# Attention scores and weighted sums as 64-by-64 products on TensorE, and half of q transposed by products with the identity

## The chip, the cores and the metric

The kernel runs on one core of a Trainium2 chip. The metric is device time in microseconds (us), the median of several runs. The core's engines are named as in the profile: PE (TensorE, matrix products into PSUM), PEld (its weight loads, which overlap PE), DVE (VectorE), ACT (ScalarE), POOL (GpSimd), and SP, whose queue issues most DMAs.

## The reference

Everything is float32. Attention runs inside chunks of 64 tokens; its output feeds a layer with one of eight experts per token, and that feeds a last dense layer.

```python
def _attn_ref(q, k, v):                       # (8, 8, 576, 64) each
    q_c = q.reshape(B, H, nc, chunk, D)       # chunk = 64, nc = 9; k_c, v_c alike
    scores = scale * np.matmul(q_c, k_c.transpose(0, 1, 2, 4, 3))
    scores = scores - np.max(scores, axis=-1, keepdims=True)
    attn = np.exp(scores)
    attn = attn / (np.sum(attn, axis=-1, keepdims=True) + 1e-09)
    out = np.matmul(attn, v_c)

def reference(**kwargs):
    attn_out = _attn_ref(q, k, v)             # -> x: 4608 tokens of 512
    x = _moe_ref(x, w_gate, w1, w2)           # argmax of x @ w_gate picks 1 of 8 experts
    return _moe2_ref(x, w_in, w_out)          # (relu(x @ w_in) ** 2) @ w_out
```

## The kernel before

Three functions run in turn: `attention()` (to about 205 us of the profiled span), `experts()` (to about 685 us) and `second()`. The change touches the first alone. Its work is cut into 36 tiles of 128 tokens (two chunks), and into 18 units of two tiles, for which q and k are loaded together. A loop `for it in range(-4, NTILE + 1)` issues one tile's steps per turn, each for another tile: `scores(it + 1)`, the first half of the transposes of q or k (`trans(..., 0)`; q in even turns, k in odd ones), `x_t` (the transpose of a finished tile), `expo(it + 1)`, the second half (`trans(..., 1)`), `pv(it - 1)` (the weighted sum), `attn_t(it)`, and in some turns `late_steps`. Every engine takes its instructions in the order in which they are written, so this loop is the order of the work; semaphores hold an engine where its input is not there.

The steps, with the names of their tiles in the profile:

- `trans`: four 128x128 transposes on PE into a PSUM tile `tq`, one for each head; line 279 then copies `tq` to SBUF with four ACT copies of 64 partitions by 256 elements. q goes to `qT`, with two heads of a pair on the two halves of the partitions. k goes to `kb`, where every pair of heads is a block matrix with zeros in the two off-diagonal blocks; these are written once by `fill_k`.
- `scores`: eight products, 128 rows by 64 columns of weights from `qT`, 128 moving columns from `kb`, into `sc` (one PSUM bank; the pool `ps_s` holds two such tiles). The zeros keep the two heads of a pair apart. DVE then takes the maximum (`mx`, line 296) and subtracts it (`at`, line 298).
- `expo` and `attn_t`: ACT takes the exponential in place (line 303), PE transposes four times into `ta`, ACT copies to `aT` (line 311).
- `pv`: eight products of 128 rows, 64 columns and 130 moving columns, `aT` against `vb`, which again holds zeros (`fill_v`) and a column of ones for the sum, into `pv`. DVE adds 1e-9, takes the reciprocal and multiplies (lines 330 to 333); SP stores the tile to DRAM.
- `x_t`: four transposes into `tx`, a DVE copy to `xT` (line 349).
- `late_steps`: for every group of four tiles, in four turns, `gate` (PE products `gl`, ACT copy `gs`), `gate_t` and `route` (eight short DVE instructions), `place` (short PE products, DVE), and `scatter` (four indirect DMAs that POOL issues, line 510).

PSUM has eight banks: four tiles of `ps_t` (for `tq`, `tx`, `ta`, `gl` and others), two of `ps_s`, two for `pv`. SBUF is handed out by tags with a fixed number of buffers; the eight `vb` tiles take six of tag `h` and one each of `b` and `a`, so three of the four `a` buffers are left for loads of q and k.

## Time and profile before

| | us |
|---|---|
| median of 3 runs (lowest, highest) | 1479.04 (1475.89, 1479.36) |
| the profiled execution | 1477.98 |
| its span, first to last instruction | 1476.2 |
| attention: from 0 to the last transposes of its tiles | about 205 |

The span leaves 1.8 us of the profiled execution outside. The granted clock of TensorE has a mean of 0.995 of full speed. Over the whole span PE is busy 97%, DVE 51%, ACT 41%, POOL 32%; these shares are means over three stages with different limits, and attention has to be read for itself.

### The profile page before, as it was taken

How to read it: one execution, taken by the hardware profiler on the slowest of the kernel's cores; microseconds unless marked ns; L12 is line 12 of the kernel's file. 1: busy time of each engine (PE TensorE's matmuls, PEld its weight loads, DVE VectorE, ACT ScalarE, POOL GpSimd, SP SyncE). 2: the span in 40 equal slices, each digit the busy share in tenths (PEclk: the TensorE clock that was granted, in tenths of full speed). 3: DMA queues.
4: the chain of work that ended last, by engine and by line, in shares of the span. 5: the costliest groups of instructions: out<-in, count | busy, mean ns of one | idle time of the engine just before them, and what ended most of it. 6: DMA issues, size and time to landing. Idle time of an engine off the chain costs nothing.

```text
span 1476.2 us, 21686 instructions
## 1 busy us (share of the span) xinstructions
PE 1429.1 (97%) x8186; PEld 1219.6 (83%) x8186; DVE 757.4 (51%) x1374; ACT 601.0 (41%) x1111; POOL 468.7 (32%) x566
## 2 busy tenths in 40 slices
PE   6999978999999999999999999999999999999998
PEld 5777758888889999998888888888888888888886
DVE  4766767768887878885532232322233232322322
ACT  7988833443444445554432222222222222222222
POOL 5335455435545545653003040120403003040201
PEclk9999999999999999999999999999999999999999
DMA  9998645757767777885301010010101001010000
GB/s 202 262 216 208 171 130 183 217 171 228 235 210 232 238 229 256 260 269 179 107 1 59 0 60 0 24 36 0 59 0 52 8 8 52 1 59 1 30 2 29
DMA packets 144370, 172.91 MB, mean 117 GB/s; under 512 B 18160, under 2 KB 103872, under 8 KB 144256
## 3 DMA queue, kind: packets, MB, share of 16 engines
q1 hardware_dynamic: 110032, 112.58, 27.0%
q0 software_dynamic: 17920, 40.51, 9.8%
q10 hardware_dynamic: 16304, 18.36, 3.8%
q8 instruction: 66, 1.08, 0.3%
q14 instruction: 48, 0.39, 0.1%
HBM read 133.05 MB, written 38.34 MB: 116 GB/s over the span
## 4 chain that ended last, share of the span: by engine, by line
PE 53%; POOL 0%; POOLq 0%; issue 0%; DVE 0%
PE hp L993 27%; PE py L1014 26%; POOL out_dram L974 0%; POOLq L1079 0%; DVE o L1022 0%; POOL between L973 0%
## 5 line engine op out<-in xcount | busy, mean ns | idle before, releaser
L993 PE MATMUL hp<-xm,w_None 128*128 128x512 f32 x1728 | 416.5, 390 | 3.1 <-DVEq L937 3.1
L993 PEld LDWEIGHTS hp<-xm,w_None 128*128 128x128 f32 x1728 | 325.4, 188 | 71.0 <-ACTq L937 3.3
L1014 PE MATMUL py<-w_None,h 128*128 128x512 f32 x1512 | 363.2, 389 | 0.0
L1014 PEld LDWEIGHTS py<-w_None,h 128*128 128x128 f32 x1512 | 283.9, 188 | 58.8
L998 DVE SCALAR_TENSOR_TENSOR rs<-hp,rs 128x512 f32<-128x512 f32 x144 | 99.6, 691 | 435.0 <-ACT rs L997 431.6
L997 ACT ACTIVATE rs<-hp 128x512 f32<-128x512 f32 x144 | 85.9, 597 | 456.6 <-PE hp L993 446.0
L755 PE MATMUL pa<-xs,w 128*128 128x256 f32 (+2 forms) x1344 | 242.5, 329 | 6.9 <-DVE h L759 2.9
L767 PE MATMUL pb<-h,w 128*128 128x256 f32 (+2 forms) x1344 | 243.9, 331 | 0.0
L974 POOL DMA_INDIRECT out_dram<-o,tp x36 | 35.1, 974 | 628.6 <-ACT o L1020 622.6
L755 PEld LDWEIGHTS pa<-xs,w 128*128 128x128 f32 x1344 | 211.4, 189 | 24.7 <-DVE h L759 4.1
L767 PEld LDWEIGHTS pb<-h,w 128*128 128x128 f32 x1344 | 209.9, 190 | 14.5
L1000 DVE TENSOR_TENSOR h<-rs,h 128x512 fp32r<-128x512 f32 x144 | 99.7, 693 | 99.0 <-ACT h L999 95.5
L758 ACT ACTIVATE h<-pa 128x256 fp32r<-128x256 f32 (+2 forms) x112 | 53.2, 475 | 217.6 <-PE pa L755 169.9
L190 DVE TENSOR_TENSOR w<-raw,w 128x1024 fp32r<-128x1024 f32 x100 | 132.7, 1328 | 17.2 <-ACT w L189 12.4
L999 ACT CAST h<-rs 128x512 fp32r<-128x512 f32 x144 | 89.4, 621 | 111.2 <-DVE rs L998 100.2
L189 ACT CAST w<-raw 128x1024 fp32r<-128x1024 f32 x113 | 118.2, 1047 | 0.0
L759 DVE SCALAR_TENSOR_TENSOR h<-pa,h 128x256 fp32r<-128x256 f32 (+2 forms) x112 | 59.6, 535 | 61.5 <-ACT h L758 49.9
L803 POOL TENSOR_TENSOR cr<-cr 128x256 f32<-128x256 f32 x64 | 50.2, 784 | 124.5 <-ACT h L758 43.3
L804 POOL TENSOR_TENSOR cr<-cr 128x256 f32<-128x256 f32 x64 | 71.5, 1117 | 5.0
L258 POOL DMA_DIRECT2D vb<-in_v_dram x64 | 46.4, 747 | 67.4 <-PE pv L321 67.3
L270 PE MATMUL tq<-ident,qk 128*128 128x128 f32 x288 | 47.7, 296 | 14.1 <-DMA qk<-in_q_dram 9.9
L279 ACT COPY qT<-tq 64x256 f32<-64x256 f32 x144 | 56.0, 389 | 10.8 <-PE tq L270 9.1
(197 smaller groups left out, 1316.0 us busy)
## 6 DMA issues: line engine op xcount, KB each, us to landing
raw<-in_moe_w_dram SPq DMA_DIRECT2D x112, 512.0 KB
x_d<-x SPq DMA_DIRECT2D x36, 256.0 KB
x<-y_d POOLq DMA_DIRECT2D x36, 256.0 KB
cr<-in_moe_w_in_dram SPq DMA_DIRECT2D x32, 256.0 KB
cr<-in_moe_w_out_dram SPq DMA_DIRECT2D x32, 256.0 KB
vb<-in_v_dram POOLq DMA_DIRECT2D x56, 144.0 KB
qk<-in_q_dram SPq DMA_DIRECT2D x12, 512.0 KB
qk<-in_k_dram SPq DMA_DIRECT2D x12, 512.0 KB
```

What stands on the lines that cost most here:

```text
L189: nc.scalar.copy(w[0], raw)
L190: eng.tensor_tensor(out=w[1], in0=raw, in1=w[0], op=ALU.subtract)
L755: nc.tensor.matmul(ps[:, 0:N], lhsT=w[wl][:, kk, o:o + 128], rhs=xT[:, xl, kk, 0:N], start=(kk == 0 and wl + xl == 0), stop=(kk == KD - 1 ...
L759: nc.vector.scalar_tensor_tensor(out=h[:, 1, 0:N], in0=ps[:, 0:N], scalar=0.0, in1=h[:, 0, 0:N], op0=ALU.max, op1=ALU.subtract)
L767: nc.tensor.matmul(pb[d][:, 0:N], lhsT=w[wl][:, f % 2, 128 * d:128 * d + 128], rhs=h[:, hl, 0:N], start=(f + hl + wl == 0), stop=(f == NF ...
L804: nc.gpsimd.tensor_tensor(out=af, in0=af, in1=ef, op=ALU.add)
L993: nc.tensor.matmul(ps, lhsT=w[wl][:, kk, o:o + 128], rhs=xT[:, xl, kk, :], start=(kk == 0 and wl + xl == 0), stop=(kk == KD - 1 and wl == 1))
L997: nc.scalar.activation(out=rs[:, 0], in_=ps, func=AF.Relu)
L998: nc.vector.scalar_tensor_tensor(out=rs[:, 1], in0=ps, scalar=0.0, in1=rs[:, 0], op0=ALU.max, op1=ALU.mult)
L999: nc.scalar.copy(h[:, 0], rs[:, 1])
L1000: nc.vector.tensor_tensor(out=h[:, 1], in0=rs[:, 1], in1=h[:, 0], op=ALU.subtract)
L1014: nc.tensor.matmul(ys[t], lhsT=h[:, hl, 128 * t:128 * t + 128], rhs=w[wl][:, g % 2, :], start=(g == 0 and hl + wl == 0), stop=(g == NF2 - ...
```

## The change

The zeros go. `kb` keeps k transposed in the same layout as `qT`: two heads of a pair on the two halves of the partitions. `scores` then makes sixteen products instead of eight, each of 64 rows (one head), 64 columns and 64 moving columns; the two heads of a pair go to two PSUM banks, and `sc` becomes two banks large, with one buffer in place of two. `pv` makes sixteen products of 64 rows, 64 columns and 65 moving columns instead of eight with 130, the heads of a pair again in two banks. `vb` has four tiles, all of tag `h`, without the zero blocks.

For the first half of q (`one = nm == "q" and hh == 0`) the four transposes are replaced by eight products with the identity, each with 64 columns of weights; each lands on the half of the partitions on which its head belongs, so that one ACT copy of 128 partitions by 512 elements replaces the four. The other half of q, and k, are transposed and copied as before.

At the start, `fill_k` and `fill_v` (36 memsets of blocks of `kb` and `vb` on DVE and POOL) go; four POOL memsets of the columns of ones remain. v of the first batch is loaded in two parts of 2 and 7 chunks instead of 6 and 3, and the first part goes ahead of the second load of q and k. The load of v's second batch is written later (at `it == 0`), but on POOL's queue it still stands right behind that of the first.

```diff
-            ps_s = actx.enter_context(tc.tile_pool(name="ps_s", bufs=2, space=PSUM))
+            ps_s = actx.enter_context(tc.tile_pool(name="ps_s", bufs=1, space=PSUM))
...
-            vb = [[tl("hhhhhhba"[4 * s + p], [128, NCB, 2, D + 1], F32, f"vb{s}{p}") for p in range(NPAIR)] for s in range(2)]
-            kb = [tl("b", [128, NPAIR, 4, 2, CH], F32, f"kb{s}") for s in range(2)]
+            vb = [[tl("h", [128, 2, NCB, D + 1], F32, f"vb{s}{z}") for z in range(NPAIR // 2)] for s in range(2)]
+            kb = [tl("b", [128, NPAIR, 128, 2], F32, f"kb{s}") for s in range(2)]
...
+                one = nm == "q" and hh == 0
                 for h in range(4):
-                    nc.tensor.transpose(ps[:, h // 2, h % 2, :], src[:, 4 * hh + h, :], ident)
+                    if one:
+                        r, p = divmod(h, 2)
+                        for j in range(2):
+                            nc.tensor.matmul(ps[64 * j:64 * j + 64, p, r, :], lhsT=src[:, 2 * p + j, 64 * r:64 * r + 64], rhs=ident, start=True, stop=True)
+                    else:
+                        nc.tensor.transpose(ps[:, h // 2, h % 2, :], src[:, 4 * hh + h, :], ident)
+                to = st["qT", u] if nm == "q" else kb[u % 2]
+                if one:
+                    nc.scalar.copy(to[:, 2 * hh:2 * hh + 2].rearrange("q p n r -> q p r n"), ps)
+                    return
...
-                ps = ps_s.tile([128, H, CH], F32, tag="s", name="sc")
+                ps = ps_s.tile([128, 2, 512], F32, tag="s", name="sc")
                 for p in range(NPAIR):
                     for c2 in range(2):
...
+                        for j in range(2):
+                            c = slice(64 * h2 + 32 * c2, 64 * h2 + 32 * c2 + 32)
+                            nc.tensor.matmul(
+                                ps[64 * c2:64 * c2 + 64, j, CH * p:CH * p + CH],
+                                lhsT=qt[64 * j:64 * j + 64, p, c].rearrange("q i r -> q (i r)"),
+                                rhs=kt[64 * j:64 * j + 64, p, c].rearrange("q i r -> q (i r)"),
...
-                            ps[64 * c2:64 * c2 + 64, p // 2, o:o + 2 * (D + 1)],
-                            lhsT=aT[:, p, 64 * c2:64 * c2 + 64],
-                            rhs=vb[b % 2][p][:, c].rearrange("p j d -> p (j d)"),
...
+                        for j in range(2):
+                            nc.tensor.matmul(
+                                ps[64 * c2:64 * c2 + 64, j, (D + 1) * p:(D + 1) * (p + 1)],
+                                lhsT=aT[64 * j:64 * j + 64, p, 64 * c2:64 * c2 + 64],
+                                rhs=vb[b % 2][p // 2][64 * j:64 * j + 64, p % 2, c],
...
-            fill_k(0)
+            for s_ in range(2):
+                for t in vb[s_]:
+                    nc.gpsimd.memset(t[:, :, :, D:D + 1], 1.0)
+            load_v(0, (nc.gpsimd, nc.sync), 0, 2)
             load_qk(1)
...
-            fill_v(1, nc.gpsimd)
-            load_v(1)
...
+                if it == 0:
+                    load_v(1)
...
```

On PE, a turn of the loop in which q is transposed reads as follows before (`qk_286` is the loaded unit, `vb_106` to `vb_109` the four pairs of heads; a shape is weight columns by moving columns):

```order
L288 MATMUL sc<-kb_114,qT_312 64x128 x8
L270 MATMUL tq<-ident,qk_286 128x128 x4
L348 MATMUL tx<-ident,x 128x128 x4
L270 MATMUL tq<-ident,qk_286 128x128 x4
L321 MATMUL pv<-vb_106,aT 64x130 x2
L321 MATMUL pv<-vb_107,aT 64x130 x2
L321 MATMUL pv<-vb_108,aT 64x130 x2
L321 MATMUL pv<-vb_109,aT 64x130 x2
L309 MATMUL ta<-ident,at 128x128 x4
```

The same turn on PE now:

```order
L296 MATMUL sc<-kb_110,qT_286 64x64 x16
L276 MATMUL tq<-ident,qk_252 64x128 x8
L358 MATMUL tx<-ident,x 128x128 x4
L278 MATMUL tq<-ident,qk_252 128x128 x4
L331 MATMUL pv<-vb_106,aT 64x65 x8
L331 MATMUL pv<-vb_107,aT 64x65 x8
L319 MATMUL ta<-ident,at 128x128 x4
```

The order of the steps stays; the first `tq` series now has the 64-column shape and stands between two series of other shapes.

On ACT, two turns (q, then k) before:

```order
L279 COPY qT_530<-tq 64x256 x4
L303 ACTIVATE at<-at 128x512
L279 COPY qT_530<-tq 64x256 x4
L311 COPY aT<-ta 128x512
L279 COPY kb_114<-tq 64x8x32 x4
L303 ACTIVATE at<-at 128x512
L279 COPY kb_114<-tq 64x8x32 x4
L311 COPY aT<-ta 128x512
```

And now:

```order
L281 COPY qT_570<-tq 128x2x2x128
L313 ACTIVATE at<-at 128x512
L285 COPY qT_570<-tq 64x256 x4
L321 COPY aT<-ta 128x512
L285 COPY kb_110<-tq 64x256 x4
L313 ACTIVATE at<-at 128x512
L285 COPY kb_110<-tq 64x256 x4
L321 COPY aT<-ta 128x512
```

One copy stands where four stood, once in two turns; nothing else moves.

On SP's queue, at the start of the program, before (`qk_129` and `qk_140` are the second and third loads of q and k):

```order
L248 DMA qk_129<-in_q_dram 128x8x128
L248 DMA qk_129<-in_k_dram 128x8x128
L258 DMA vb_106<-in_v_dram 64x6x64
L258 DMA vb_107<-in_v_dram 64x6x64
L258 DMA vb_108<-in_v_dram 64x6x64
L258 DMA vb_109<-in_v_dram 64x6x64
L248 DMA qk_140<-in_q_dram 32x8x128
```

And now (`qk_135` and `qk_138` are the second and third loads):

```order
L259 DMA vb_106<-in_v_dram 64x2x64 x2
L259 DMA vb_107<-in_v_dram 64x2x64 x2
L249 DMA qk_135<-in_q_dram 128x8x128
L249 DMA qk_135<-in_k_dram 128x8x128
L249 DMA qk_138<-in_q_dram 32x8x128
```

Two of the nine chunks of v moved ahead of the second load of q and k, and the other seven behind the third.

## Rows read from the trace of the kernel before

**Rows 1.** Stretches: us, busy PE, PEld, DVE, ACT, POOL, then clock, DMA share, GB/s.

```profile
35.42:81.80 46.38, 45.76 (x510) 35.73 (x509) 31.91 (x71) 43.64 (x103) 15.95 (x24) 1.00 1.07 261
81.80:178.55 96.75, 89.77 (x1003) 69.77 (x1001) 67.07 (x172) 83.34 (x196) 44.87 (x72) 1.00 0.85 202
178.55:205.24 26.69, 17.21 (x187) 13.14 (x186) 17.73 (x45) 9.49 (x17) 16.99 (x18) 0.94 0.37 103
111.42:131.97 20.55, 18.89 (x211) 14.60 (x210) 13.55 (x33) 17.48 (x42) 11.51 (x21) 1.00 0.96 216
```

**Rows 2.** Timeline of ACT, plain tile: start, us, engine, line, op, count [idle before].

```profile
39.42 0.63 ACT L303 ACTIVATE at<-at 128x512 f32<-128x512 f32 x1
...
40.06 1.58 ACT L279 COPY kb<-tq 64x256 f32<-64x256 f32 x4
...
41.67 0.59 ACT L311 COPY aT<-ta 128x512 f32<-128x512 f32 x1
...
42.15 1.59 ACT L279 COPY qT<-tq 64x256 f32<-64x256 f32 x4
...
43.77 0.63 ACT L303 ACTIVATE at<-at 128x512 f32<-128x512 f32 x1
```

**Rows 3.** Groups by form, 0 to 320 us: busy us, mean ns of one | idle before.

```profile
L279 ACT COPY qT<-tq 64x256 f32<-64x256 f32 x144 | 56.0, 389 | 10.8 <-PE tq L270 9.1
...
L311 ACT COPY aT<-ta 128x512 f32<-128x512 f32 x36 | 21.1, 585 | 7.6 <-PE ta L309 3.9 <-PE tq L270 3.0
...
L778 ACT COPY y<-pb 128x256 f32<-128x256 f32 x4 | 1.2, 392 | 0.0
...
L356 PEld LDWEIGHTS gl<-xT,wg 128*32 128x32 f32 x64 | 1.3, 108 | 1.3 <-issue 1.2 <-ACT kb L279 0.2
```

**Rows 4.** Timeline of weight loads and products, one turn with a gate.

```profile
111.42 0.85 PEld L288 LDWEIGHTS sc<-kb,qT 128*64 128x64 f32 x16 [0.17 <-issue]
...
112.44 0.42 PEld L270 LDWEIGHTS tq<-ident,qk 128*128 128x128 f32 x4 [0.17 <-issue]
...
112.83 0.47 PEld L348 LDWEIGHTS tx<-ident,x 128*128 128x128 f32 x4
...
113.91 0.86 PEld L321 LDWEIGHTS pv<-vb,aT 128*64 128x64 f32 x16 [0.17 <-ACT aT L311]
...
114.94 0.42 PEld L309 LDWEIGHTS ta<-ident,at 128*128 128x128 f32 x4 [0.17 <-issue]
...
115.53 0.16 PEld L356 LDWEIGHTS gl<-xT,wg 128*32 128x32 f32 x8 [0.17 <-issue]
115.53 1.06 PE L356 MATMUL gl<-xT,wg 128*32 128x512 f32 x8
...
116.53 0.85 PEld L288 LDWEIGHTS sc<-kb,qT 128*64 128x64 f32 x16 [0.84 <-issue]
116.53 1.09 PE L288 MATMUL sc<-kb,qT 128*64 128x128 f32 x16
```

**Rows 5.** Timeline, the same turn: POOL's first scatter and the maximum on DVE.

```profile
116.81 1.04 POOL L510 DMA_INDIRECT tk_d<-tok,pos  x1 [0.27 <-issue]
...
118.87 0.69 DVE L296 TENSOR_REDUCE mx<-sc 128x8 f32<-128x512 f32 x1 [2.68 <-PE tx L348]
```

**Rows 6.** Timeline, the turn behind a route: DVE on `sc`, and the next scores.

```profile
125.56 0.68 DVE L296 TENSOR_REDUCE mx<-sc 128x8 f32<-128x512 f32 x1
...
126.28 0.69 DVE L298 TENSOR_TENSOR at<-sc,mx 128x512 f32<-128x512 f32 x1
...
126.44 0.85 PEld L288 LDWEIGHTS sc<-kb,qT 128*64 128x64 f32 x16
```

**Rows 7.** Timeline of the start: v of the second batch, and k's transposes of unit 2.

```profile
14.36 5.83 POOL L258 DMA_DIRECT2D vb<-in_v_dram  x8
...
27.56 1.56 PE L270 MATMUL tq<-ident,qk 128*128 128x128 f32 x8 [3.40 <-DMA qk<-in_k_dram]
...
31.74 0.85 PEld L288 LDWEIGHTS sc<-kb,qT 128*64 128x64 f32 x16 [0.17 <-issue]
```

## The prediction

> **What bounds the kernel now.** I read the page first: PE is busy 97% of the span, but the change touches only attention, the first 205 us, so I read the busy times by stretch. They split attention into four parts [rows 1]. Until 35 us it waits for loads. From 35.4 to 81.8 us there are 11 tiles with almost no routing, 46.38/11 = 4.22 us each, with ACT busy 43.64 of 46.38 us. From 81.8 to 178.55 us there are 19 tiles with a routing group for every four, 96.75/19 = 5.09 us each. In the last 27 us no transposes of q or k are left, and every engine idles a lot.

> In the plain part ACT sets the pace: its exponentials begin at 39.42 and 43.77, 4.35 us apart, and between them stand two series of four copies (1.58 and 1.59 us), the copy to `aT` and the exponential, end to end [rows 2]. In the part with groups no engine is full. In the four tiles from 111.42 to 131.97 (20.55 us) PE is busy 18.89, ACT 17.48, DVE 13.55 [rows 1]. PE comes nearest; 20.55 - 18.89 = 1.66 us are waits. One source of them shows in rows: the scores that begin at 116.53 are done 1.09 us later, at 117.62, but DVE, idle for 2.68 us, takes their maximum only at 118.87, while POOL issues the scatters [rows 4, 5]. I cannot explain these 1.25 us from the dependences, and the change does not touch the scatters, so I leave the group's waits as they are.

> PE's own prices come from the starts of its series [rows 4]: scores 111.42 to 112.44, 1.02 us, of which 0.17 us is the pause at the change of shape; four transposes 112.44 to 112.83, 0.39 us; `pv` 113.91 to 114.94, 1.03 us. Scores are 16 records of 128 moving columns in 0.85 us, transposes one record per 128 columns at about 0.1 us: so two score records, on the two column halves, run side by side, and the series is eight steps of 0.106 us. The gate's products show four column strips at once: eight records of 512 columns in 1.06 us.

> **The change part by part.**

> *Scores and `pv` in quarters (gain on PE).* Each series becomes 32 records with half the moving columns (64 of 128, 65 of 130). If the two row halves run side by side as the column halves do, four records run at once, and the series is eight steps half as long: 0.85/2 = 0.43 us saved, and I take 0.40 for the start of the series. No row shows two row halves at work. From above the bound is 0.43 us; from below it is nothing (halves in turn: 16 steps of half length). I take a value near the upper end, since the nearest row, the gate's, shows the array shared by four strips. A tile saves 2 x 0.40 = 0.80 us of PE, a group of four 3.2 us.

> *Half of q by products (loss on PE, gain on ACT).* Per unit, four transposes (0.39 us) become eight products with 64 weight columns and 128 moving columns. That is the form and count of the old scores, 1.02 us with the change of shape that now stands behind it: +0.63 us a unit, 1.26 us a group. On ACT four copies of 389 ns (1.59 us as a series) become one of 128 x 512. The nearest row is the copy to `aT`, 585 ns [rows 3]. That the new one writes every second element should not matter: a 64 x 256 copy that does so takes 389 ns, and a 128 x 256 copy without gaps 392 ns [rows 3]. Bounds: 0.585 and, at two old copies' price, 0.78 us. I take 0.585: 1.0 us saved per unit, 2.0 us a group.

> *Sum per group of four with routing:* PE 18.89 - 3.2 + 1.26 = 16.95 us; ACT 17.48 - 2.0 = 15.5; DVE 13.55. PE stays nearest, and with the old 1.66 us of waits the group takes 18.6, so 1.94 us less. For 19 tiles: 19/4 x 1.94 = 9.2 us.

> *Plain part:* ACT 4.35 - 0.5 = 3.85 us a tile; PE needs, from the starts above without the gate, about 4.1 - 0.80 + 0.32 = 3.6, so ACT stays the bound. 11 x (4.22 - 3.85) = 4.1 us.

> *One buffer for the scores (loss).* The next scores must now wait until DVE has subtracted the maximum. In most turns this is long done: DVE's two instructions take about 1.4 us, and PE's other series stand for 3 us and more between the end of one scores and the start of the next, 112.44 to 116.53 [rows 4]. Behind a route it is not: the subtraction runs from 126.28 to 126.97, the next scores began at 126.44 [rows 6], so 0.53 us late, once a group. The scores are then 0.4 us shorter, which covers most of it. From nothing to 0.53 us for about five groups; I take 1.3 us in all.

> *Last 27 us:* the tiles alternate PE, DVE and ACT there; shorter scores and `pv` sit on that chain once or twice: 1.0 us gained, between 0 and 2.

> *Start.* The memsets on DVE and POOL go, but nothing waited for them. What held the start is data: k's transposes for unit 2 stood idle 3.40 us until 27.56 for their load, and the steady part begins with the scores of 31.74 and 35.42 [rows 7]. POOL issued v of the second batch from 14.36 [rows 7]; without the memsets it issues it some 6 us sooner, so it competes earlier with q and k, while on SP seven of nine chunks of v's half move behind unit 2. The bytes that go ahead of unit 2 stay about the same. I take 0, within 2 us either way.

> *Buffers.* With `vb` out of tag `a`, q and k have four buffers. Loads are not what PE waits for after 35 us, so nothing.

> Sum: -9.2 - 4.1 + 1.3 - 1.0 = -13.0 us. Against the profiled execution, 1477.98 us, that gives 1465.0; the median, 1479.04, lies 1.1 us above it. What attention gains is kept: the stage behind it is bound by PE from about 210 us on, with its first weights loaded long before.

> **The rivals.**

> *Slower: the row halves run in turn.* Then scores and `pv` keep their 0.85 us, and the products for q cost PE 1.26 us a group: 19/4 x 1.26 = +6.0 us; in the plain part PE rises to about 4.1 + 0.32 = 4.4 us a tile against 4.22, +1.5; the single buffer +1.3: 1487. It decides from a saving under 0.16 us a series (1.26/8). For it: nothing in this trace uses row halves. Against it: column strips do run at once, and the heads of a pair now go to separate banks. 10%. [...]

> *About as fast, or a little slower: a floor under the distance of two starts.* 32 records must start in 0.43 us, one each 13 ns; at 27 ns nothing of the 0.85 us is gained. The gate's eight weight loads of 108 ns all lie within 0.16 us, so they start (160 - 108)/7 = 7 ns apart [rows 3, 4]. [...] 5%. [...]

> *Less gain: the waits grow.* PE, ACT and DVE come within 3.4 us of each other per group, and each late signal, as at 118.87, now meets one score buffer. If the groups keep half of their gain and the plain part all, -4.6 - 4.1 + 2.5 = -6: 1472. 18%.

> *More gain:* if ACT's relief also removes half of the groups' waits (0.8 us each), 1459 or less. 7%.

> **How the numbers follow.** Forecast 60% (1459 to 1470), less gain 18% (1470 to 1477), floor 5%, slower 10%, more gain 7%. The likeliest is 1465. The range 1457 to 1477 leaves out most of the two slow cases and the far end of the good one. A measurement of this kernel tells 0.3% (4.4 us) from no change, so the border is at 1474.6: faster 0.60 + 0.07 + two thirds of 0.18 = 0.78; same, from the rest of that case and half the floor case, 0.09; slower 0.13.

> **What would show it.** Scores of 32 records in about 0.45 us and `pv` alike, against 0.85 if the halves take turns; the first `tq` series of q at about 0.85 us; 18 copies of about 585 ns; exponentials about 3.85 us apart in the plain part; four tiles with routing in about 18.6 us; the last transposes of attention's tiles near 190 us instead of 204, and everything behind it shifted by the same amount. I am wrong if scores still take 0.85 us, if a wait of scores for DVE's subtraction stands in most turns, or if the plain part begins later than 36 us.

## The result, and the profile after

The changed kernel is slower: 1492.5 us (median; the profiled execution 1489.2, its span 1487.4) against 1479.2, a ratio of 1.009 with a 95% interval of 1.0067 to 1.0113. The forecast was 1465.

What the change does to single series came out as forecast. The timeline of the changed kernel, plain part (start, us, engine, line, op, count [idle before]); lines here are those of the changed kernel: scores L296, `mx` L305, `at` L307, exponential L313, `aT` L321, `pv` L331, `rc` L340, products of q L276, transposes L278, the one copy L281, scatters L503:

```profile
36.72 0.56 PEld L296 LDWEIGHTS sc<-kb,qT 64*64 64x64 f32 x32 [0.17 <-issue]
36.73 0.69 PE L296 MATMUL sc<-kb,qT 64*64 64x64 f32 x32
...
38.81 0.56 PEld L331 LDWEIGHTS pv<-vb,aT 64*64 64x64 f32 x32 [0.17 <-issue]
38.81 0.70 PE L331 MATMUL pv<-vb,aT 64*64 64x65 f32 x32
...
40.64 0.85 PEld L276 LDWEIGHTS tq<-ident,qk 128*64 128x64 f32 x16
...
42.53 0.65 ACT L281 COPY qT<-tq 128x512 f32<-128x512 f32 x1
```

Against [rows 4] the loads of a scores series take 0.56 us in place of 0.85 and its products 0.69 in place of 1.09, so I take it that the two row halves do run side by side. One load record lasts 0.14 us and one product record 0.22, so 32 loads start on average (0.56 - 0.14)/31 = 14 ns apart and 32 products (0.69 - 0.22)/31 = 15 ns; in this series they start in fours, 6 to 7 ns apart, and the next four 35 to 39 ns later (once, between two products, 87). The products of q take the 0.85 us that were expected. The exponentials show the plain part at its new pace:

```profile
39.79 0.63 ACT L313 ACTIVATE at<-at 128x512 f32<-128x512 f32 x1
...
43.04 0.64 ACT L313 ACTIVATE at<-at 128x512 f32<-128x512 f32 x1
...
47.27 0.63 ACT L313 ACTIVATE at<-at 128x512 f32<-128x512 f32 x1
...
50.52 0.63 ACT L313 ACTIVATE at<-at 128x512 f32<-128x512 f32 x1
```

They are 3.25 and 4.23 us apart in turn, where [rows 2] has 4.35. Then it goes wrong. The same engines in the same stretches as in [rows 1], and the end of attention in both kernels (the changed one first; us, busy PE, PEld, DVE, ACT, POOL, then clock, DMA share, GB/s):

```profile
35.42:81.80 46.38, 39.71 (x873) 32.25 (x873) 31.12 (x69) 37.84 (x87) 15.98 (x24) 0.98 1.04 258
81.80:178.55 96.75, 84.59 (x1705) 67.34 (x1701) 65.69 (x166) 71.93 (x163) 45.00 (x72) 0.96 0.84 202
...
186.00:220.00 34.00, 21.09 (x270) 14.15 (x268) 17.25 (x40) 8.72 (x14) 16.98 (x18) 0.70 0.38 111
```

```profile
186.00:220.00 34.00, 23.85 (x187) 18.62 (x186) 21.39 (x57) 11.83 (x18) 17.56 (x25) 0.95 0.42 125
```

No engine is full. PE has saved work (84.59 us busy where it had 89.77), but in the same stretch of 96.75 us it waits longer, and the granted clock is 0.96 where it was 1.00. The starts of exponentials and of the first expert product (us from the start of the span) cut the loss into parts:

| us | before | changed | difference in the stretch that ends there |
|---|---|---|---|
| 4th exponential | 35.1 | 35.5 | +0.4 |
| 12th exponential | 70.4 | 70.6 | -0.2 |
| 32nd exponential | 172.0 | 174.8 | +2.6 |
| first expert product | 209.7 | 219.6 | +7.1 |
| end of the span | 1476.2 | 1487.4 | +1.3 |

What PE waits for is in its groups, 35 to 205 us (busy us, mean ns | idle before, and its releasers), the changed kernel first and then `pv` before, by tile:

```profile
L296 PE MATMUL sc<-kb,qT 64*64 64x64 f32 x1024 | 28.0, 233 | 11.9 <-issue 8.4 <-DVE at L307 3.3
L331 PE MATMUL pv<-vb,aT 64*64 64x65 f32 x1088 | 26.4, 233 | 7.0 <-issue 6.6 <-ACT aT L321 0.4
```

```profile
L321 PE MATMUL pv<-vb,aT x544: 274/274/326, 38.0 to 198.4; 128*64 128x130 f32 x182
...
  issue: 0.3, 1
```

15 us stand ahead of scores and `pv` as "issue": PE waited for nothing that the profile shows. Before, it was 0.3 us. Two kinds of places hold them. The first, in the timeline of all engines:

```profile
53.95 0.57 PE L331 MATMUL pv<-vb,aT 64*64 64x65 f32 x21
...
57.35 0.45 PE L331 MATMUL pv<-vb,aT 64*64 64x65 f32 x11 [2.83 <-issue]
...
57.83 0.17 DVE L340 TENSOR_SCALAR rc<-pv 128x8 f32<-128x8 f32 x1 [3.12 <-PE pv L331]
...
58.41 0.59 ACT L321 COPY aT<-ta 128x512 f32<-128x512 f32 x1 [1.42 <-PE ta L319]
```

PE stops after 21 of the 32 records of one series, all of whose inputs are there, and goes on 2.83 us later; DVE and ACT stand still behind it. Count all records of PE from 0 in order of their starts: weight loads, products and the 137 short instructions of its sequencer, which are mostly waits for semaphores. The record behind this stop is then number 1473. Seven more records that start over 0.3 us behind the one ahead of them, with nothing that released them, stand at 1217, 1729, 1985, 3265, 4033, 4289 and 4801: all eight are 193 plus a multiple of 256. The queues on the page say what comes in such portions (packets, MB), changed and before:

```profile
q8 instruction: 77, 1.26, 0.3%
```

```profile
q8 instruction: 66, 1.08, 0.3%
```

1.26 MB in 77 packets are 16.4 KB each. The two traces have 19245 and 16545 records of PE, 75.2 and 64.6 times 256, for 77 and 66 packets. From these counts I estimate that one packet holds the next 256 instructions of PE, a block. I call this a **stop at a block**. Its length goes with the moment at which the block's packet starts. In this trace it started 0.07 us after PE had used up the block before: stop of 3.04 us from start to start; 0.58 us ahead: 2.11; 1.55 us ahead: 1.33; 2.04 us ahead: 0.78; 2.26 us ahead: 0.20; 2.8 us or more ahead: none beyond the 0.17 us of a change of shape. The records behind the eight stops start 2.5 to 3.0 us after the transfer of their blocks does (the transfer lasts 1.1 to 1.5 us), and in the kernel before, counted alike, most transfers start 7 to 12 us ahead of the first record of their block. The changed kernel has about 172 PE instructions a tile instead of about 100, and uses 256 of them mostly in 5 to 7 us, where nothing stops it, instead of 10 to 13. Between 30 and 205 us its stops sum to 12.6 us, those of the kernel before to nothing. One stop seems to cost more than its length: behind that of 2.88 us, which ends at 134.62, the granted clock is 0.50 of full speed until 138.0. Between the 4th and the 32nd exponential the changed kernel spends 10.2 us at that level, the kernel before none.

The second kind, while POOL issues a group's scatters:

```profile
74.34 1.06 POOL L503 DMA_INDIRECT tk_d<-tok,pos  x1 [1.40 <-DVE mx L305]
...
74.77 0.70 PE L331 MATMUL pv<-vb,aT 64*64 64x65 f32 x32
...
77.36 0.33 PE L296 MATMUL sc<-kb,qT 64*64 64x64 f32 x4
...
77.85 0.35 PE L296 MATMUL sc<-kb,qT 64*64 64x64 f32 x5 [0.16 <-issue]
...
78.27 0.96 POOL L503 DMA_INDIRECT tk_d<-tok,pos  x1 [0.21 <-issue]
...
78.58 0.33 PE L296 MATMUL sc<-kb,qT 64*64 64x64 f32 x4 [0.38 <-issue]
...
80.00 0.92 PE L296 MATMUL sc<-kb,qT 64*64 64x64 f32 x19 [1.08 <-issue]
...
80.06 0.17 DVE L340 TENSOR_SCALAR rc<-pv 128x8 f32<-128x8 f32 x1 [4.53 <-remote]
```

`pv` is done at 75.47, but DVE takes it only at 80.06, 1.8 us after the start of the fourth scatter. Meanwhile PE starts only four or five products, with as many weight loads, every 0.7 us: the scores take 3.6 us instead of 0.69. I call this the **hold**. The kernel before has it too: the late maximum at 118.87 [rows 5] is one, and such late maxima are gone from the part with groups where the scatters are taken out of it (below).

### The profile page after: what moved, and what is told of

It reads as the page before. It is cut to its first block, busy times and chain, and to the rows that moved or that the text cites. A ratio compares the mean times of both kernels' runs of the same rounds, so it can differ in the third digit from the quotient of the medians.

```text
span 1487.4 us, 24319 instructions
## 1 busy us (share of the span) xinstructions
PE 1422.9 (96%) x9554; PEld 1216.8 (82%) x9554; DVE 750.6 (50%) x1354; ACT 582.7 (39%) x1057; POOL 466.6 (31%) x554
## 3 DMA queue, kind: packets, MB, share of 16 engines
q8 instruction: 77, 1.26, 0.3%
## 4 chain that ended last, share of the span: by engine, by line
PE 53%; POOL 0%; POOLq 0%; issue 0%; DVE 0%
PE hp L986 27%; PE py L1007 26%; POOL out_dram L967 0%; POOLq L1072 0%; DVE o L1015 0%; POOL between L966 0%
## 5 line engine op out<-in xcount | busy, mean ns | idle before, releaser
L285 ACT COPY kb<-tq 64x256 f32<-64x256 f32 x144 | 55.8, 387 | 12.6 <-PE tq L278 9.6
L223 POOL DMA_INDIRECT xg<-x_d,tk x40 | 46.0, 1150 | 27.2 <-PE pt L737 16.2
```

## The experiments

The experiments fell on four chips. On one the kernel before takes 1465.5 us, on the others 1479 to 1482. In the traces of the first I saw no hold: with scores or `pv` alone in quarters, and the scatters in place, the 20 tiles from the 12th to the 32nd exponential take 91.1 and 91.0 us there, where the kernel before takes 101.6 in the trace of [rows 1]. On the others it is there where a group's scatters run back to back between the tiles: in the second traces of the two kernels, changed and before, DVE goes on with `pv` only 1.6 and 1.9 us after the start of a group's fourth scatter. "With the hold" and "without the hold" stand for these two kinds of chips below. Every ratio is against the kernel before on the same chip. "Stops" are those at blocks, summed from 30 to 205 us. A trace is one execution; the two traces of the changed kernel differ by 9 us at the 34th exponential, so small differences between single traces show little.

**Each part alone, put into the kernel before** (chip without the hold). Scores in quarters, with one buffer of two banks (the products alone are shown, of a longer edit):

```diff
-                        nc.tensor.matmul(
-                            ps[64 * c2:64 * c2 + 64, 2 * p:2 * p + 2, :],
+                        for j in range(2):
+                            nc.tensor.matmul(
+                                ps[64 * c2:64 * c2 + 64, j, CH * p:CH * p + CH],
```

> The kernel before with one part of the change alone: scores in 64 by 64 quarters, with kb in its new layout (no zeros, no fill_k) and sc in two banks with one buffer. pv and q's transposes are as before. Theory A (PE's instructions arrive too slowly: the change gives PE about 170 instructions a tile instead of about 100, and its series stop in the middle, 256 instructions apart, with nothing to wait for): about half of the added instructions are here, so there are a few stops in the middle of series, in all 3 to 8 us of idle time of PE without a releaser, against 0.3 us before and about 16 us in the changed kernel; the saving on PE, about 0.3 us a tile, is about eaten up: within 6 us of the kernel before. Theory B (the single buffer for the scores is the loss): the whole loss is here, 8 us or more slower, and PE's idle time ahead of the scores names DVE's subtraction.

Measured: 1464.6, ratio 0.9995 (0.9985 to 1.0004), three stops, 2.9 us. Then `pv` alone (shown likewise):

```diff
-                        nc.tensor.matmul(
-                            ps[64 * c2:64 * c2 + 64, p // 2, o:o + 2 * (D + 1)],
+                        for j in range(2):
+                            nc.tensor.matmul(
+                                ps[64 * c2:64 * c2 + 64, j, (D + 1) * p:(D + 1) * (p + 1)],
```

> The kernel before with one part of the change alone: pv in 64 by 64 quarters, with vb in its new layout (no zeros, only the columns of ones are set; loads in the old order). Scores with two buffers and q's transposes are as before. Theory A (instructions arrive too slowly): the same count of added instructions as in the run with quartered scores alone, so the same 3 to 8 us of stops in the middle of series; within 6 us of the kernel before. Theory B (the single buffer is the loss): no loss here, the 0.3 us a tile that PE saves show as 4 to 8 us faster.

Measured: 1465.3, ratio 0.9997 (0.9987 to 1.0006), three stops, 3.7 us. Theory B falls with these two. In the plain part the exponentials stay 4.35 us apart in both: ACT is the bound, so what PE saves alone brings nothing. Nor does it in the part with groups: from the 12th to the 32nd exponential these two take 91.1 and 91.0 us, and the kernel before, its scatters moved away (below), 91.1. Half of q by products alone:

```diff
+                if nm == "q" and hh == 0:
+                    for h in range(4):
+                        r, p = divmod(h, 2)
+                        for j in range(2):
+                            nc.tensor.matmul(ps[64 * j:64 * j + 64, p, r, :], lhsT=src[:, 2 * p + j, 64 * r:64 * r + 64], rhs=ident, start=True, stop=True)
+                    nc.scalar.copy(st["qT", u][:, 2 * hh:2 * hh + 2].rearrange("q p n r -> q p r n"), ps)
+                    return
```

> The kernel before with one part of the change alone: half of q by products with the identity and one copy in place of four. Scores and pv are as before. It adds 24 PE instructions a unit, 12 a tile, 0.63 us of PE a unit, and takes 1.0 us of ACT a unit away. Theory A (instructions arrive too slowly): few stops, under 3 us; the plain part gains up to 0.25 us a tile (ACT 4.35 to 3.85, PE 4.1 to 4.4), the part with routing loses up to 0.3 us a tile: between 3 us faster and 6 us slower. Theory B (the single buffer is the loss) says the same. If this alone is 10 us slower, both theories fall.

Measured: 1470.2, ratio 1.0028 (1.0018 to 1.0037), no stops from 35 to 198 us. PE is now full: 96.73 of the 96.75 us from 81.80 to 178.55. Alone, then, no part gains: the first two save on PE while ACT sets the pace, and the third relieves ACT but fills PE. More instructions without any of the change (the line stands once ahead of the scores and, into an unread column, once ahead of `pv`):

```diff
+                for z in range(8):
+                    nc.tensor.matmul(ps[32 * (z % 4):32 * (z % 4) + 32, 0, 0:1], lhsT=ident[:, 0:32], rhs=ident[:, 0:1], start=True, stop=True)
```

> The kernel before with sixteen more products a tile on PE, each of 32 weight columns of the identity and one moving column, eight ahead of the scores (into sc, overwritten by the scores) and eight ahead of pv (into columns of the bank that nothing reads): 64 more PE instructions a tile, as many as the change adds in scores and pv, but no other change. Judging from the gate's eight weight loads in 0.16 us, eight such products should take PE 0.2 to 0.4 us with the pauses at the change of shape. Theory A (instructions arrive too slowly): stops without a releaser in the middle of series, in sum 8 to 20 us in attention as in the changed kernel (before: 0.3 us), and 256 instructions apart; 15 us or more slower. Theory B (single buffer) and a theory by which the 64-row products themselves are at fault: no such stops, only the price of the tiny products, at most 0.8 us a tile on PE, partly within its waits.

Measured: 1480.5, ratio 1.0097 (1.0080 to 1.0114), but one stop of 1.7 us after 35 us, not 8 to 20; the rest is the price of the products on PE, which is busy 95.30 of 96.75 us. So the count of instructions alone is not it. Two things differ from the changed kernel. A block of 256 instructions lasts 7.2 us (median, 35 to 165 us), as these take PE time, where it lasts 5.6 in the changed kernel on the same chip (the last run below); and a block's transfer starts 1.5 us (median) after PE enters the block ahead of it, there 3.4. So 19 of its 22 transfers start 4 us or more ahead. Which of the two counts for more, and why the transfers start sooner, was not tried.

**The two kernels again** (a chip with the hold).

> The changed kernel itself, once more, on the chip of these runs. In the four runs before this one the kernel before took 1465.6 us, against 1479.2 us beside which the changed kernel was measured, and its parts put into the kernel before showed only two to four stops of PE in the middle of a series, each 0.7 to 1.7 us. Theory A (instructions arrive too slowly, as a property of the kernel): the stops are here as in the first trace, about 16 us of PE's idle time without a releaser, and the kernel is again about 13 us slower than the kernel before. Theory C (the instruction blocks and PE's signals are late in some executions or on some chips, and the changed kernel suffers more from that): where the kernel before takes 1466 us, the stops sum to 3 to 8 us, and the changed kernel is between 8 us faster and 4 us slower. Theory B (single buffer) says slower by 8 us or more, with PE waiting for DVE's subtraction ahead of most scores.

Measured: 1491.5, ratio 1.0077 (1.0052 to 1.0102); stops 12.8 us.

> The kernel before itself, for its trace on the chip of these runs. Theory A expects the trace of before as it was, only shorter by about 13 us somewhere that none of the theories names. Theory C expects that the 13 us are gone from attention: exponentials 4.35 us apart through the part with routing too, without the turns of 5.8 to 6.5 us, and the first expert products near 197 us instead of 209.7.

Measured: 1479.7; its trace is like the first one's, with turns of 5.91 and 5.81 us at the second and third group and the first expert product at 209.8; no stops. The chip is one with the hold, so theory C had to be tried otherwise (below).

**Parts of the changed kernel** (same chip). q transposed as before:

```diff
-                one = nm == "q" and hh == 0
+                one = False
```

> The changed kernel with both halves of q transposed and copied as before the change: 24 PE instructions fewer a unit, 0.63 us of PE less and 1.0 us of ACT more a unit. Theory A: a few stops fewer than in the changed kernel, but ACT is the bound again at 4.35 us a tile in the plain part, so it loses there what it gains: within 5 us of the changed kernel. Theory C: ACT's 4.35 us a tile hold everywhere, so the kernel takes what the kernel before takes, within 4 us, and is slower than the changed kernel by 2 to 8 us.

Measured: 1489.2, ratio 1.0063 (1.0041 to 1.0086), stops 5.4 us. Fewer instructions, fewer stops, and ACT again at 4.34 us a tile, as theory A expected; but with less than half of the stops it is still 9 us slower than the kernel before, so on this chip the stops are not all. Without most loads of v (`pv` then reads old values, so the routing behind it and the time of the whole, 2075 us, are others, and only attention can be compared):

```diff
-                    if hi > lo and lo + 2 < B:
-                        load_v(lo + 2)
```

> The changed kernel without the loads of v for six of the eight batches: pv goes on with v of the first two, so from the third batch on the values are others, and with them the routing. It takes about 7 MB of the transfers and 48 of POOL's DMA issues out of attention. Theory A, and C where the blocks are late because they share the DMA engines with the loads: blocks of instructions land in 0.9 us instead of up to 1.5, and the stops in the middle of series shrink to under a third. If the stops stay as they are, the load on the DMA engines is not their cause.

Measured: stops 1.3 us, where the changed kernel has 12.6 and 12.8, so most of the stops go with the loads of v. But the 34th exponential comes at 187.4, no earlier than in the changed kernel (186.8 and 195.9 in its two traces). The holds remain: the turns with scatters take 7.2 to 8.3 us, as they did with the stops (7.3 to 8.0 in the first trace).

**The hold.** One scatter a turn instead of four, in both kernels (another chip with the hold):

```diff
-                    if w == 0 or g < NG0:
+                    if step is scatter and g < NG0 - 1:
+                        for j in range(4):
+                            late.setdefault(t + w + j, []).append((lambda g, get, j=j: scatter(g, get, j), g))
+                    elif w == 0 or g < NG0:
```

> The changed kernel, with the four scatters of a group issued one a turn in four turns instead of four in one turn (the last group before the first gather excepted). In the traces in which the kernel before takes 1479 us, PE's signals to the other engines are held from POOL's first scatter until about 1.9 us after the start of the fourth, 5.7 us in all, and PE itself starts only about ten instructions every 0.7 us meanwhile; in the traces in which the kernel before takes 1466 us neither is seen. Theory D (the loss is this hold, in which 32 products take twice as many steps as 16, and one score buffer is used up sooner): where the hold exists, four short holds of about 1.9 us are mostly covered, the groups fall to under 20.5 us, and the kernel is 10 us or more faster than the changed kernel's 1491, thus 1481 or less. Where no hold exists this kernel is about what the changed kernel is there, and by theory D that is faster than the kernel before by 5 us or more. Theory A (instruction blocks that come too late, alone): the scatters do not matter, 1491 within 4 us, and still slower than the kernel before where no hold exists.

> The kernel before with the same edit: one scatter a turn. Theory D: where the hold exists, the kernel before loses about 3 us a group to it (turns of 5.9 and 5.8 us instead of 4.4), and gets most of that back: 8 to 13 us faster, near 1467. Where no hold exists: within 3 us of the kernel before. Theory A alone: within 3 us on either.

Measured: 1491.7, ratio 1.0074 (1.0053 to 1.0095), and 1481.1, ratio 0.9997 (0.9986 to 1.0009). No answer, as the edit did not do what it says in the first groups, and only in part in the later ones. POOL's timeline in the kernel before with spread scatters, second group:

```profile
98.16 1.04 POOL L513 DMA_INDIRECT tk_d<-tok,pos  x1 [0.27 <-issue]
...
99.51 0.99 POOL L513 DMA_INDIRECT tk_d<-tok,pos  x1 [0.21 <-issue]
...
100.81 0.96 POOL L513 DMA_INDIRECT tk_d<-tok,pos  x1 [0.21 <-issue]
...
102.07 0.96 POOL L513 DMA_INDIRECT tk_d<-tok,pos  x1 [0.22 <-issue]
```

Written in four turns, they still run back to back: nothing that they wait for stands between them. On the same chip, one score buffer alone, and `pv` alone once more:

```diff
-            ps_s = actx.enter_context(tc.tile_pool(name="ps_s", bufs=2, space=PSUM))
+            ps_s = actx.enter_context(tc.tile_pool(name="ps_s", bufs=1, space=PSUM))
```

> The kernel before with one buffer of one bank for the scores instead of two, and nothing else: the price of that part alone. Theory B (the single buffer is the loss): 8 us or more slower. Theory D: where the hold exists the next scores now wait until the hold ends, 1 to 1.5 us a group more and some 3 us in the tail: 5 to 12 us slower; where no hold exists under 3 us slower. Theory A alone: under 3 us slower on either.

Measured: 1482.2, ratio 1.0008 (0.9995 to 1.0022). In the kernel before, the buffer costs next to nothing even with the hold; theory B falls, and theory D's 5 to 12 us with it.

> The kernel before with pv alone in quarters, as in the second run, on the chip of these runs. If the hold exists here: theory D expects some loss from the 32 more instructions a tile that fall into the hold, but two score buffers: 0 to 6 us slower than the kernel before (it was 0.4 us faster where no hold exists). Theory B: faster by some us, as pv is shorter and the scores keep two buffers. If no hold exists here: within 3 us, as in the second run.

Measured: 1483.6, ratio 1.0016 (1.0004 to 1.0029), one stop of 2.2 us. In its trace the 34th exponential comes at 186.6, where the kernel before has 182; where the hold is absent the same edit cost nothing. Of the 4.6 us the stop is 2.2; so more instructions seem to make a hold dearer by themselves.

Then the scatters of all groups were moved to the last group's turn, behind the 34th exponential, which is the time to compare (the whole is longer, 1519.4 and 1509.0 us in single runs, as POOL's scatters now stand ahead of the first gather):

```diff
-                        late.setdefault(t + w, []).append((step, g))
+                        late.setdefault(4 * NG0 + 5 if step is scatter else t + w, []).append((step, g))
```

> The changed kernel with the scatters of all groups issued together with the last group's, at the end of attention. The end of attention itself becomes later by POOL's 28 scatters of 1.3 us; what counts is the time of the 34th exponential, before them (171 to 187 us in the changed kernel, 182 in the kernel before). Theory D (the hold during the scatters makes the loss): no turns of 7.2 to 9 us are left but those with a stop at a block of instructions, four tiles with routing take 19 us or less, and the 33rd exponential comes 15 us or more earlier than in the changed kernel. Theory A (stops at blocks of instructions make the loss): the turns with scatters get shorter, but the stops at blocks remain at 10 us or more in sum and the 33rd exponential comes less than 8 us earlier.

> The kernel before with the same edit, as its comparison: no holds, no stops at blocks. Four tiles with routing take 3 times 4.36 and once 4.86 us, 17.9 us, where they took 20.5; the 33rd exponential comes 10 to 13 us earlier than in the kernel before. Theory D expects the changed kernel with this edit to reach its 33rd exponential earlier than this one; theory A expects it later.

> The changed kernel with the scatters at the end of attention and without the loads of v for six of the eight batches (values and routing are others from the third batch on). Both disturbances away: if stops and hold together make the loss, four tiles with routing take 3.48 + 3.75 + 4.23 us and one turn behind the route of 5.5 us, 17.0 us, about 1 us less than in the kernel before with late scatters, and the 33rd exponential comes at least 5 us earlier than in that kernel. If it is not earlier, a third cause (the one score buffer behind the route) eats the gain.

> The kernel before with the scatters at the end of attention and without the loads of v for six of the eight batches (values and routing are others from the third batch on): the comparison for the changed kernel with both edits, whose 34th exponential came at 163.7 us. Theory A: the kernel before has no stops at blocks, so the loads cost it nothing, and its 34th exponential comes at 172.8 us within 3 us, as with late scatters alone. If it comes 8 us or more earlier, the loads of v cost both kernels, in some other way than by stops at blocks.

| kernel | scatters | loads of v | 34th exponential, us | stops, us |
|---|---|---|---|---|
| before | in place | all | 182.4, 182.0 | 0 |
| before | late | all | 172.8 | 0 |
| before | late | two batches | 172.8 | 0 |
| changed | in place | all | 186.8, 195.9 | 12.6, 12.8 |
| changed | in place | two batches | 187.4 | 1.3 |
| changed | late | all | 179.3 | 16.6 |
| changed | late | two batches | 163.7 | 5.6 |

The last two rows differ by 15.6 us, and the loads cost the kernel before nothing: 172.8 either way. Of the 15.6 us, 2.3 stand ahead of the 4th exponential (36.6 against 34.3), and 11.8 between the 12th and the 32nd: 95.3 us against 83.5 for the same 1817 product records. There the stops fall from 11.1 to 0.5 us. So without the hold the stops, with the low clock behind some of them, take the changed kernel's whole gain there, 91.1 - 83.5 = 7.6 us, and 4.2 us more. Three kernels in one stretch (changed with late scatters; changed with both away; before with late scatters), columns as above:

```profile
81.80:165.00 83.20, 74.78 (x1582) 61.13 (x1572) 61.68 (x155) 65.76 (x150) 23.31 (x32) 0.96 0.98 236
```

```profile
81.80:165.00 83.20, 79.03 (x1791) 63.80 (x1789) 70.48 (x180) 75.88 (x172) 1.73 (x1) 1.00 0.63 179
```

```profile
81.80:165.00 83.20, 83.08 (x959) 66.38 (x959) 64.55 (x166) 79.69 (x188) 23.31 (x32) 1.00 0.98 236
```

With both away the changed kernel passes 1791 product records where it passed 1582, at full clock, and ACT does more work (75.88 us) with PE at 79.03. The kernel before with late scatters, one group and the next, shows what a group's pace is without the hold:

```profile
99.42 0.63 ACT L303 ACTIVATE at<-at 128x512 f32<-128x512 f32 x1
...
103.88 0.63 ACT L303 ACTIVATE at<-at 128x512 f32<-128x512 f32 x1
...
108.25 0.63 ACT L303 ACTIVATE at<-at 128x512 f32<-128x512 f32 x1
...
112.62 0.63 ACT L303 ACTIVATE at<-at 128x512 f32<-128x512 f32 x1
...
117.48 0.63 ACT L303 ACTIVATE at<-at 128x512 f32<-128x512 f32 x1
```

Three turns keep close to ACT's 4.35 us of the plain part, and the turn with the gate takes 4.86. Last, the scatters written one a turn as above and each held back by a wait for DVE's last instruction of `pv`, in both kernels (in the changed kernel the second line differs in its layout):

```diff
-            nc.gpsimd.memset(between[0:1, t % 16:t % 16 + 1], 0)
+            m = nc.gpsimd.memset(between[0:1, t % 16:t % 16 + 1], 0)
+            if j is not None:
+                tc.add_manual_dep(m.ins, E["pace"].ins.name, mybir.DependencyInfo(mybir.DependencyClass.Sync, mybir.DependencyReason.DATA),
+                                  reason="one a turn")
...
-                nc.vector.tensor_tensor(out=x, in0=pv_[:, :, :, 0:D], in1=rc.to_broadcast([128, 2, 4, D]), op=ALU.mult)
+                E["pace"] = nc.vector.tensor_tensor(out=x, in0=pv_[:, :, :, 0:D], in1=rc.to_broadcast([128, 2, 4, D]), op=ALU.mult)
```

> The kernel before with one scatter a turn, and now each held back by a wait for DVE's last instruction of pv in its turn, so that they cannot run back to back (the last group's stay together). Theory D: a hold of about 1.9 us a turn is within what PE, ACT and DVE have in hand, so the groups fall from 20.5 toward 18 us: 6 to 12 us faster than the kernel before where the hold exists. If the short holds stop the engines each time: 4 holds of 1.9 us instead of one of 5.7, and the kernel is as slow as before or slower by up to 5 us. Where no hold exists: within 3 us.

Measured, on a chip with the hold: 1473.5 against 1482.0, ratio 0.9944 (0.9923 to 0.9965); the 34th exponential at 172.4. So this kernel is faster than the kernel before, by 8.5 us; on the chip without the hold it was not run. Its scatters in one group, the first two still 1.3 us apart and the others in turns of their own:

```profile
94.51 1.04 POOL L516 DMA_INDIRECT tk_d<-tok,pos  x1 [0.27 <-issue]
...
95.85 0.99 POOL L516 DMA_INDIRECT tk_d<-tok,pos  x1 [0.22 <-issue]
...
100.01 0.96 POOL L516 DMA_INDIRECT tk_d<-tok,pos  x1 [0.16 <-issue]
...
104.81 0.96 POOL L516 DMA_INDIRECT tk_d<-tok,pos  x1 [0.16 <-issue]
```

> The changed kernel with one scatter a turn, each held back by a wait for DVE's last instruction of pv in its turn, as in the kernel before with paced scatters (8.5 us faster than before, 34th exponential at 172.4). Theory A (stops at blocks of instructions make the loss): 10 us or more of stops remain, the 34th exponential comes at 178 to 184 us and the time is 1479 to 1487, slower than the kernel before with the same edit by 6 us or more. Theory D (the hold made the loss): the 34th exponential comes before 170 us and the time is under 1470.

Measured, on the chip without the hold: 1474.7 against 1465.5, ratio 1.0074 (1.0047 to 1.0100); stops 17.2 us, the 34th exponential at 178.2. I saw no hold in this trace while the tiles run (in the stop below DVE takes `pv` 0.09 us behind its last product, 113.06 to 113.15), and the changed kernel is still 9 us slower: theory D falls as the only cause, and so does theory C, by which the stops would be few here (3 to 8 us) and the kernel about as fast as the kernel before; theory A stands. One of its stops:

```profile
109.97 0.68 PE L331 MATMUL pv<-vb,aT 64*64 64x65 f32 x26
...
112.72 0.34 PE L331 MATMUL pv<-vb,aT 64*64 64x65 f32 x6 [2.08 <-issue]
...
113.15 0.17 DVE L340 TENSOR_SCALAR rc<-pv 128x8 f32<-128x8 f32 x1 [2.82 <-PE pv L331]
```

**What is settled, and what is not.** Without the hold the stops make the loss: with late scatters, taking the loads away takes them away and brings the gain, and on the chip without the hold the changed kernel with paced scatters has 17.2 us of stops and is slower. (The changed kernel as it stands was not run on that chip, nor the kernel before with paced scatters.) On chips with the hold, either alone takes the gain (187.4 and 179.3, against 182 and 172.8), and the two do not add up: with both it is 186.8 and 195.9. Why they overlap so was not tried. Nor was it settled why a chip has the hold or not, or what makes a transfer of instructions start when it does; that it starts sooner with fewer loads is shown (from 35 to 165 us a median of 2.0 us after PE enters the block ahead of it, against 3.1 with all loads, both with late scatters).

## Why the prediction was wrong

*Scores and `pv` in quarters: right in size.* I took 0.40 us a series; from its start to that of the next series, scores take 0.63 us (36.72 to 37.35) in place of 1.02, and `pv` 0.62 (38.81 to 39.43) in place of 1.03. The rival by which row halves run in turn fell: 32 loads take 0.56 us and 32 products 0.69. So did the floor under the distance of two starts, which no run shows: where 27 ns would have left nothing of the gain, the trace has 14 to 15 ns on average.

*Half of q by products: right on PE (0.85 us), a little low on ACT:* the copy takes 0.64 to 0.65 us, where I took the 0.585 of [rows 3]. Whether the writing to every second element makes the difference, which I had ruled out, was not tried.

*The plain part: the pace right, the stretch wrong.* From the 4th to the 9th exponential a tile takes (54.8 - 35.5)/5 = 3.86 us; forecast 3.85, before 4.35. Then the stops of 3.04, 0.65 and 0.99 us, up to 70.5 us, give nearly all of it back.

*The groups: here the sum failed.* The forecast had -9.2 us; the 20 tiles from the 12th to the 32nd exponential took 2.6 us more than before. The sum costed a series by what the array does and had no term for its instructions: "Each series becomes 32 records" stood in the text, and only the array's steps of them had a price. What it left out is the stops, 11.1 us over these tiles where the hold is away. With stops and hold both nearly away, the 20 tiles take 83.5 us in the changed kernel (70.9 to 154.4) and 91.1 in the kernel before (72.1 to 163.2): 16.7 and 18.2 us a group. The gain of 1.5 us a group is near the forecast 1.94, and 16.7 is near the 16.95 that I had computed for PE alone.

That is partly luck. I took PE as nearest to the bound because it was busy 18.89 of 20.55 us; but a group of the kernel before takes only 18.2 us without the hold, so the 18.89 held time in which PE's records were drawn out. And without the hold ACT sets the pace of three turns in four there, too, as the exponentials above show: what scores and `pv` save on PE alone gained nothing (91.1 and 91.0 us), and the one copy for ACT alone cost time, because its products fill PE. The gain needs all of them.

*"I leave the group's waits as they are": wrong, and the second gap.* The late signal of [rows 5] was in the text with its 1.25 us and no cause. It is the hold, which costs the group of [rows 1] 20.55 - 18.2 = 2.3 us. A wait that I could not explain had no right to the same price in a kernel with 1.7 times the instructions: here its effect grows with them. In the kernel before, second trace, the scores in a hold:

```profile
100.30 1.35 PE L288 MATMUL sc<-kb,qT 128*64 128x128 f32 x16
```

That is 0.26 us more than the 1.09 of [rows 4]; the changed kernel's scores at 77.36 take 2.9 us more than the 0.69 of the plain part, five times their time in all.

*One score buffer: right.* Forecast 1.3 us; alone, in the kernel before, 0.3 us by the medians (-0.7 to +3.3 by the ratio).

*The end of attention: forecast -1.0, measured +7.1.* The stretch is that from the 32nd exponential to the first expert product. Tiles depend on each other there; PE idles, and its granted clock is at 0.50 for 20.5 of the 34 us from 186 to 220. From the timeline of PE, changed kernel:

```profile
189.63 0.66 PE L319 MATMUL ta<-ident,at 128*128 128x128 f32 x4
192.79 1.13 PE L296 MATMUL sc<-kb,qT 64*64 64x64 f32 x32 [2.50 <-DVE at L307]
```

Scores take 1.13 us in place of 0.69 behind 2.50 us of idleness; the granted clock from 186 to 220 us is 0.70 of full speed on average, where it was 0.95: from 192.7 to 202.9 and from 206.3 to 216.6 it is 0.50, against 3.4 us at that level before. Other traces tell something of the cause. With the hold the stretch takes 44.8 and 47.5 us in the changed kernel and 37.7 and 38.0 in the kernel before; without it 36.0 in the changed kernel with paced scatters and 33.3 to 36.3 in the kernel before with a part of the change. So most of the loss seems to come with the hold. How it divides between hold, clock and buffer was not tried apart. *The start* came within the 2 us (+0.4).

The forecast named as a sign of error "if a wait of scores for DVE's subtraction stands in most turns". It does not (3.3 us in all); the error was none of my rivals. "Less gain: the waits grow" was nearest, and bounded the growth by half of the gain. Two of the rivals' sums were also off, without weight for the forecast: in the slower case the plain part adds 11 x (4.4 - 4.22) = 2.0 us, not 1.5, and half of the groups' waits taken from 1465 leaves 1461, not 1459.

## What to carry to other kernels

Cutting products into smaller ones that share the array multiplies PE's instructions (here about 100 a tile before, 172 after), and by my reading these have to be brought in: compare the time in which PE uses up 256 of them (here 10 to 13 us before, 5 to 7 after) with the time from the start of an instruction packet to its first record where PE stood for it (here 2.5 to 3.0 us), and look for idle "issue" time in the middle of a series (here 15 us, before 0.3). A wait in the trace of before that no dependence explains is a price still unknown; find what it scales with before it is carried over. And look in the trace whether an engine's work stands in the turns in which it is written: POOL's scatters, written in four turns with nothing to wait for, ran 1.3 us apart; pacing them by a wait was worth 8.5 us in the kernel before, on a chip with the hold.
